# Four norm and score steps one slot later, and the last chunk's joined-sum products in another order

## The chip, the core and the metric

The kernel runs on one core of a Trainium2 chip. The metric is the device time of one execution in microseconds (us), as the median of several runs. Before the change it is 802.1 us, the median of four runs: 802.75, 802.56, 801.64 and 801.57 us.

The engines are named as in the profile: PE (matrix products; its weight loads are PEld), DVE (vector), ACT (scalar functions and copies), POOL (general elementwise work, and issuing of some transfers) and SP (issuing of transfers only). Each engine works through its own instructions in order; engines wait for one another through semaphores.

## What is computed

Two parts in sequence: an attention over channels, and a gated feed-forward layer on its result.

```
qn = q / (norm of q over N + 1e-6);  kn likewise       # q, k, v: 4 x 6016 x 256
s  = kn.T @ qn / tau;  s = s - max;  a = exp(s);  a /= a.sum(-1) + 1e-9   # 4 x 256 x 256
x  = (v @ a) as 24064 x 256
out = (sigmoid(x @ w_gate) * (x @ w_val)) @ w_out       # w_gate, w_val: 256 x 1536; w_out: 1536 x 256
```

So per batch there is a 256 x 256 matrix `a`, and the product `v @ a @ w_gate` can be had as `v @ (a @ w_gate)`: the kernel folds `a` into the weights once per batch.

## The kernel before

**Tiling.** A batch has 47 row tiles of 128 rows. They are taken in 12 chunks (`ci` 0 to 11), eleven of four tiles (512 rows) and a last one of three (384 rows). A chunk has 12 slots (`f` 0 to 11), one for each 128 of the 1536 hidden features. All four batches run one after the other, so there are 4 x 12 x 12 = 576 slots.

**One slot** (`glu`, L640 on). PE makes `ps_gate` (two matmuls), then a share of the product work for the chunk before (`run_work`), then `ps_val` (two matmuls). ACT turns `ps_gate` into `g_sb` (L660). DVE joins `g_sb` with `ps_val` into `hT` (L663). `ps_gate` and `ps_val` have two buffers each, so the `ps_val` matmuls of a slot need the L663 of two slots before.

**Products with fewer multiplications.** For a chunk of four tiles, `hT @ w_out` is made from seven block products instead of eight (a Strassen scheme), for two pairs `p` = 0 and 1 of tiles. The products read either `hT` itself or sums of its blocks. `a_sum` (L674) makes these *joined sums* on DVE, for each half of the features in three steps: step 0 (L689, the diagonal sum, read by product `z1`), step 1 (L691, read by `x2` and `y2`) and step 2 (L693, the differences, read by `z2` and `v2`). The first half's steps run in slots 7, 9 and 11 of the chunk itself (`OWN_SLOTS`), the second half's in slots 0, 2 and 4 of the next chunk (`NEXT_SLOTS`). Slots 1, 3, 5, 6, 8 and 10 have no joined sum.

`ORDER` is the order of the fourteen products (seven for each pair), six matmuls each, 84 in all; `run_work` deals them out over the next chunk's slots, seven to a slot, and about eight to a slot in the very last chunk. After `z1` of a pair, `part` (L742 to L744) copies three blocks out of PSUM on ACT and adds them on POOL; after `v2`, `whole` (L749 to L760) does the rest. Products `x2`, `y2`, `z2` and `v2` are added onto the blocks that `part` has read, so they have to come after its copy.

**The next batch's attention.** `side_work` puts steps for batch `n = b + 1` into slots of batch `b` by a slot number 0 to 143 (chunk times 12 plus slot). With `s0` = 98 the end of this chain, for `n` = 2 and 3, is: norms and a reciprocal square root (slots 105 on, DVE and POOL); `norms_inv` (L506 and L507 on DVE, 128x4) and `spread_both` (a DVE transpose, L458, and two POOL transfers `row<-rT`, L461) in slot 110; `read_row` (an SP transfer `rk_sb<-row`, L469) and `score_blocks` (eight POOL adds, L415) in slot 112; `scale_x` (L445, DVE) in slots 120 and 122; `exps` (L548, ACT) in 123 and 124; `all_sums` (five small matmuls into `ps_r` and a DVE reciprocal, L573) in 126; then twelve pieces of folded weights (`gh`: two matmuls into `ps_gh`, stored by ACT L607 or DVE L609) from slot 128 on. For `n` = 1 `norms_inv` is in slot 108 and `spread_both` in 109, there is no `score_blocks`, and the rest is the same. Slot 108 is slot 0 of chunk 9, slot 120 is slot 0 of chunk 10.

In a slot the instructions are issued in this order: `glu` with the products, the store of the chunk before last (slot 4 only), the joined sum of the slot, then the side work. All of this order is written out by hand.

Of the kernel before, what the change touches and what calls it, by code (L numbers as in the profile page):

```python
# [39 lines left out]
ORDER = (  # L40
    (0, "y1"), (1, "y1"), (0, "x1"), (0, "z1"), (1, "x1"), (1, "z1"),
    (0, "x2"), (0, "y2"), (0, "z2"), (0, "v2"),
    (1, "x2"), (1, "y2"), (1, "z2"), (1, "v2"),
)
NEXT_SLOTS = {0: 0, 2: 1, 4: 2}

FREE_SLOTS = (1, 3, 5, 6, 8, 10)
SCORE_SLOTS = {0: (1, 3, 6, 8, 10), 4: (2, 4, 6, 9, 11), 8: (0, 2, 5, 7, 10)}
GH_SLOTS = (128, 130, 131, 133, 135, 137, 138, 140, 142, 145, 147, 149)
OWN_SLOTS = {7: 0, 9: 1, 11: 2}  # L50


# [1 line left out]
def kernel(  # L54
# [26 lines left out]
    B, N, C = q.shape  # L81
# [592 lines left out]
    def a_sum(b, ci, g, m):  # L674

        nt = groups[ci][1]
        half = nt // 2
        hT = hts[b, ci]
        if (b, ci, g) not in sums:
            sums[b, ci, g] = spool.tile(  # L680
                [P, 5, FC // 4, CH // 2], BF16, tag=f"s{g}", name="sums", bufs=2 - g
            )
        f0, f1 = g * (FC // 2), (g + 1) * (FC // 2)
        n = half * P
        first, count = A_STEPS[m]
        out = sums[b, ci, g][:, first : first + count, :, :n].rearrange("p m j n -> p j m n")
        x = hT[:, f0:f1, : 2 * n].rearrange("p (j k) (r n) -> p j k r n", k=2, r=2)
        if m == 0:
            nc.vector.tensor_tensor(out=out[:, :, 0], in0=x[:, :, 0, 0], in1=x[:, :, 1, 1], op=ALU.add)  # L689
        elif m == 1:  # L690
            nc.vector.tensor_tensor(out=out, in0=x[:, :, 0], in1=x[:, :, 1], op=ALU.add)  # L691
        else:
            nc.vector.tensor_tensor(out=out, in0=x[:, :, :, 0], in1=x[:, :, :, 1], op=ALU.subtract)  # L693
# [9 lines left out]
    def out_work(b, ci):  # L703

        nt = groups[ci][1]
        half = nt // 2
        hT = hts[b, ci]
        work = []
        states = [{} for _ in range(half)]
        singles = {}  # L710
        plain = (b, ci) == (0, 0)

        def product(p, name, i):
            state = states[p]
            region, a, w = PRODUCTS[name]
            first = name == "y1" and i == 0
            if first:
                state["ps"] = pso.tile([P, CH], FP32, tag="o", name="ps_o")
            g, j = divmod(i, FC // 4)
            if isinstance(a, tuple):  # L720
                lhsT = hT[:, 2 * i + a[1], ds((a[0] * half + p) * P, P)]
            else:
                lhsT = sums[b, ci, g][:, a, j, ds(p * P, P)]
            rhs = w_out_sb[:, 2 * i + w[0], ds(w[1] * P, P)] if isinstance(w, tuple) else w_sums[:, w, i, :]
            mm(
                state["ps"][:, ds(region * P, P)],
                lhsT,
                rhs,
                start=first,
                stop=(i == FC // 2 - 1),  # L730
                skip_group_check=True,
            )
            if i == FC // 2 - 1:
                if name == "z1":
                    part(p)
                elif name == "v2":
                    whole(p)

        def part(p):

            m = states[p]["m"] = mpool.tile([P, 3, P], FP32, tag="m", name="m_sb")
            nc.scalar.copy(m, states[p]["ps"][:, : 3 * P].rearrange("p (n c) -> p n c", c=P))  # L742
            nc.gpsimd.tensor_tensor(out=m[:, 1, :], in0=m[:, 1, :], in1=m[:, 2, :], op=ALU.add)  # L743
            nc.gpsimd.tensor_tensor(out=m[:, 2, :], in0=m[:, 1, :], in1=m[:, 0, :], op=ALU.add)  # L744

        def whole(p):

            o = out_tile(b, ci)
            nc.scalar.copy(  # L749
                o[:, p : p + half + 1 : half, :],  # L750
                states[p]["ps"].rearrange("p (t c) -> p t c", c=C),
            )
            blocks = o.rearrange("p t (h c) -> p (t h) c", c=P)
            c00, c11 = 2 * p, 2 * (half + p) + 1
            ends = blocks[:, c00 : c11 + 1 : c11 - c00, :]
            mids = blocks[:, c00 + 1 : c11 : max(1, c11 - c00 - 2), :]
            last = (b, ci) == (B - 1, NCH - 2)
            add = nc.gpsimd.tensor_tensor
            add(out=ends, in0=ends, in1=states[p]["m"][:, 1:3, :], op=ALU.add)  # L759
            add(out=ends, in0=ends, in1=mids, op=ALU.subtract)  # L760
            if last:
                t0 = groups[ci][0]
                nc.sync.dma_start(out=out_rows[b][:, t0 + p : t0 + nt : half, :], in_=o[:, p:nt:half, :])
            elif p == half - 1:
                stores.append((b, ci))

        def single(s, f):
            if f == 0:
                singles[s] = pso.tile([P, CH], FP32, tag="o", name="ps_o")
            ps = singles[s]  # L770
            mm(ps[:, :C], hT[:, f, ds(s * P, P)], w_out_sb[:, f, :], f == 0, f == FC - 1)
            if f == FC - 1:
                nc.scalar.copy(out_tile(b, ci)[:, s, :], ps[:, :C])
                if plain and s == nt - 1:
                    stores.append((b, ci))

        if plain:
            return [(2, single, t, f) for t in range(nt) for f in range(FC)]
        for p, name in ORDER:
            if p < half:  # L780
                for i in range(FC // 2):
                    work.append((1, product, p, name, i))
                if nt % 2 and name == "z1":
                    for f in range(FC):
                        work.append((2, single, nt - 1, f))
        return work
# [126 lines left out]
    def side_work(b):  # L913
# [4 lines left out]
        def at(slot, fn, *a):  # L918
            side.setdefault(divmod(slot, FC), []).append((fn, a))
# [14 lines left out]
        n = b + 1  # L934
# [35 lines left out]
        if b == 0:  # L970
            at(s0 - 4, acc_fold, n, 0, (2, 1))
            at(s0 + 1, acc_fold, n, 1, (2, 1))
            at(s0 + 3, norms_mm, n)
            at(s0 + 4, root_seed, n)
            at(s0 + 4, root_steps, n)
            at(s0 + 10, norms_inv, n)
            at(s0 + 11, spread_both, n)
            at(s0 + 13, read_row, n)
        else:
            at(s0 - 4, acc_fold, n, 1, (4,))  # L980
            at(s0 - 1, acc_fold, n, 1, (2, 1))
            at(s0 + 3, acc_fold, n, 0, (4,))
            at(s0 + 4, acc_fold, n, 0, (2, 1))
            at(s0 + 5, score_out, n, 0)
            at(s0 + 7, norms_mm, n)
            at(s0 + 7, score_out, n, 1)
            at(s0 + 7, root_seed, n)
            at(s0 + 7, root_steps, n)
            at(s0 + 12, norms_inv, n)
            at(s0 + 12, spread_both, n)  # L990
            at(s0 + 14, read_row, n)
            at(s0 + 14, score_blocks, n)
        at(s0 + 22, scale_x, n, 0)
        at(s0 + 24, scale_x, n, 1)
        at(s0 + 25, exps, n, 0)
        at(s0 + 26, exps, n, 1)
        at(s0 + 28, all_sums, n)
        at(s0 + 28, gh_tiles, n)
        for i, piece in enumerate(gh_order):
            slot = GH_SLOTS[i]  # L1000
# [17 lines left out]
    for b in range(B):  # L1018
        side = side_work(b)
        for ci in range(NCH):  # L1020
            final = (b, ci) == (B - 1, NCH - 1)
            for f in range(FC):
                mid = gh_mid.get(f) if (b, ci) == (0, 0) else None
                if prev is not None:
                    mid = lambda: run_work(work, 1 / max(1, FC - final - f))
                elif mid is not None:
                    mid = lambda ns=mid: gh_pieces(ns)
                glu(b, ci, f, mid)
                if prev is not None:
                    if f == 4:  # L1030
                        store()
                    if f in NEXT_SLOTS and prev != (0, 0):
                        a_sum(*prev, 1, NEXT_SLOTS[f])
                if f in OWN_SLOTS and not final and (b, ci) != (0, 0):
                    a_sum(b, ci, 0, OWN_SLOTS[f])
                for fn, a in spill.get((b, ci, f), []) + side.get((ci, f), []):
                    fn(*a)
                if (b, ci) == (0, 0):
                    gh_pieces(gh_end.get(f, ()))
            prev = (b, ci)  # L1040
            if not final:
                work = out_work(*prev)
# [39 lines left out]
```

## Time and profile before

The profiled execution took 802.75 us, of which the span from its first to its last instruction is 800.7 us; 2.05 us lie around it. Its TensorE clock was granted at 0.998 of full speed.

| what | value |
|---|---|
| median of four runs | 802.1 us (801.57 to 802.75) |
| profiled execution | 802.75 us |
| its span | 800.7 us |
| DVE busy | 682.0 us (85% of the span) |
| ACT busy | 512.7 us (64%) |
| POOL busy | 408.8 us (51%) |
| one L663 of 512 columns, mean | 683 ns |
| one joined sum of step 0, 1, 2, mean | 559, 953, 1072 ns |
| L506 of `r_wide`, three of them | 689 to 696 ns |
| L507, L458 | 178, 209 ns |
| L445 from PSUM (batch 1), from SBUF (batches 2, 3) | 473 ns, 670 to 945 ns |

The busy share of an engine is an average; what a step costs is read from the slot it stands in. A useful yardstick is the distance between the first `ps_gate` matmuls of two neighbouring slots. In the timeline an idle time in front of an instruction is in square brackets with what ended it.

### The profile page before, as it was taken

To read this page: it belongs to the slowest core of one execution; us is meant where nothing else is said; L and a number is where in the kernel's file an instruction comes from. 1 tells how busy PE (TensorE), PEld (TensorE's weight loads), DVE (VectorE), ACT (ScalarE), POOL (GpSimd) and SP (SyncE) were. 2 spreads that over 40 slices of the span, in tenths; PEclk is the share of its full clock that TensorE was granted. 3 is DMA by queue.
4 is the path that set the end of the run, shared out by engine and by line. 5 is a ranking of instruction groups with operands and counts; after the bars stand their busy time and mean duration, and the time that the engine had idled before them with its cause. 6 is when DMAs were issued, how large, how long until landed. Compare 5 with 4: busy or idle time off the path is not lost.

```text
span 800.7 us, 18098 instructions
## 1 busy us (share of the span) xinstructions
PE 781.9 (98%) x6875; PEld 498.8 (62%) x6875; DVE 682.0 (85%) x1056; ACT 512.7 (64%) x891; POOL 408.8 (51%) x633
## 2 busy tenths in 40 slices
PE   4899999999999999999999999999999999999998
PEld 2546666666666666666666666666666666666666
DVE  5767898898889999899989999999888888888885
ACT  3766777766667767665667776766665565565563
POOL 3566455346553666554843565654754234334333
PEclk9999999999999999999999999999999999999999
DMA  9997858532685897752486599856234423423302
GB/s 214 189 205 123 139 96 141 95 66 54 131 142 105 148 180 149 138 101 53 101 147 123 103 177 164 152 114 107 54 65 86 68 54 83 78 54 81 72 27 73
DMA packets 85303, 89.12 MB, mean 111 GB/s; under 512 B 52704, under 2 KB 58464, under 8 KB 85216
## 3 DMA queue, kind: packets, MB, share of 16 engines
q0 software_dynamic: 28144, 49.82, 37.2%
q1 hardware_dynamic: 56496, 37.30, 21.2%
q8 instruction: 53, 0.87, 0.4%
q10 hardware_dynamic: 576, 0.85, 0.3%
q14 instruction: 34, 0.28, 0.1%
HBM read 79.04 MB, written 24.64 MB: 129 GB/s over the span
## 4 chain that ended last, share of the span: by engine, by line
PE 94%; DMA 4%; POOL 1%; DVE 0%; issue 0%; POOLq 0%; DVEq 0%
PE ps_val L129 30%; PE ps_gate L129 30%; PE ps_o L129 27%; PE ps_s L129 4%; DMA qk_sb<-in_k_dram 3%; PE ps_gh L129 2%; DMA w_gate<-in_moe_w_gate_dram 1%; POOL w_gate L208 0%; POOL w_val L208 0%; POOL qk_sb L148 0%; PE ps_end L129 0%; DVE hT L663 0%; POOL v_sb L160 0%; DVE sums L689 0%; DVE sums L693 0%
## 5 line engine op out<-in xcount | busy, mean ns | idle before, releaser
L660 ACT ACTIVATE g_sb<-ps_gate 128x512 f32<-128x512 f32 (+1 forms) x576 | 338.4, 588 | 248.9 <-PE ps_gate L129 237.7
L663 DVE SCALAR_TENSOR_TENSOR hT<-g_sb,ps_val 128x512 bf16<-128x512 f32 (+1 forms) x576 | 385.9, 672 | 98.5 <-PE ps_val L129 69.7
L129 PE MATMUL ps_gate<-vT,gh_G 128*128 128x512 bf16 (+1 forms) x1152 | 337.6, 375 | 0.0
L129 PE MATMUL ps_val<-vT,gh_H 128*128 128x512 bf16 (+1 forms) x1152 | 337.5, 375 | 0.1
L129 PEld LDWEIGHTS <-sums 128*128 128x128 bf16 x2670 | 183.0, 98 | 82.4 <-DVE sums L689 0.3
L759 POOL TENSOR_TENSOR out_sb<-out_sb,m_sb 128x256 f32<-128x256 f32 x89 | 69.1, 777 | 202.5 <-ACT out_sb L749 175.0
L129 PEld LDWEIGHTS <-gh_G 128*128 128x128 bf16 x1152 | 104.2, 98 | 82.3 <-DVE gh_G L609 0.3
L129 PE MATMUL ps_o<-w_sums,sums 128*128 128x128 bf16 x1602 | 154.6, 219 | 0.2 <-DVE sums L689 0.2
L129 PEld LDWEIGHTS <-hT 128*128 128x128 bf16 x1200 | 88.4, 98 | 46.8
L743 POOL TENSOR_TENSOR m_sb<-m_sb 128x128 f32<-128x128 f32 x89 | 49.6, 557 | 130.0 <-ACT m_sb L742 129.8
L760 POOL TENSOR_TENSOR out_sb<-out_sb 128x256 f32<-128x256 f32 x89 | 93.4, 1049 | 7.0
L129 PE MATMUL ps_o<-w_out_sb,sums 128*128 128x128 bf16 x1068 | 96.2, 219 | 0.0
L129 PE MATMUL ps_o<-w_sums,hT 128*128 128x128 bf16 x1068 | 95.5, 219 | 0.0
L693 DVE TENSOR_TENSOR sums<-hT 128x1536 bf16<-128x1536 bf16 (+1 forms) x92 | 95.5, 1038 | 0.0
L129 PEld LDWEIGHTS <-gh_H 128*128 128x128 bf16 x1152 | 90.2, 98 | 3.7 <-DVE gh_H L609 0.3
L691 DVE TENSOR_TENSOR sums<-hT 128x1536 bf16<-128x1536 bf16 (+1 forms) x92 | 85.6, 931 | 0.0
L129 PEld LDWEIGHTS <-qk_sb 128*128 128x128 bf16 x286 | 30.3, 106 | 42.6 <-issue 9.6
L749 ACT COPY out_sb<-ps_o 128x512 f32<-128x512 f32 x89 | 51.7, 580 | 0.0
L689 DVE TENSOR_TENSOR sums<-hT 128x768 bf16<-128x768 bf16 (+1 forms) x92 | 51.6, 561 | 0.0
L744 POOL TENSOR_TENSOR m_sb<-m_sb 128x128 f32<-128x128 f32 x89 | 46.3, 521 | 7.0
L129 PE MATMUL ps_s<-qk_sb 128*128 128x256 bf16 (+1 forms) x194 | 36.1, 308 | 13.9 <-ACT qk_sb L195 7.0
L256 ACT ACTIVATE sq<-qk_sb 128x1024 bf16<-128x1024 bf16 (+3 forms) x36 | 35.7, 1011 | 12.0 <-DMA qk_sb<-in_k_dram 12.0
(104 smaller groups left out, 552.8 us busy)
## 6 DMA issues: line engine op xcount, KB each, us to landing
out_dram<-out_sb SPq DMA_DIRECT2D x43, 512.0 KB, 3.4
v_sb<-in_v_dram POOLq DMA_DIRECT2D x44, 256.0 KB, 5.4
acc<-sq POOLq DMA_DIRECT2D x36, 256.0 KB, 4.9
qk_sb<-in_q_dram POOLq DMA_DIRECT2D x35, 256.0 KB, 7.3
qk_sb<-in_k_dram POOLq DMA_DIRECT2D x35, 256.0 KB, 6.2
qk_sb<-in_q_dram POOLq DMA_DIRECT2D x4, 512.0 KB, 11.6
qk_sb<-in_k_dram POOLq DMA_DIRECT2D x4, 512.0 KB, 13.5
w_f<-in_moe_w_out_dram POOLq DMA_DIRECT2D x3, 512.0 KB, 10.9
```

What stands on the lines that cost most here:

```text
L129: nc.tensor.matmul(out, lhsT=lhsT, rhs=rhs, start=start, stop=stop, **kw)
L256: nc.scalar.activation(out=sq[:, :nt, :], in_=src[:, :nt, :], func=ACT.Square)
L660: nc.scalar.activation(out=g_sb[:, :n], in_=ps_gate[:, :n], func=ACT.Tanh, scale=0.5)
L663: nc.vector.scalar_tensor_tensor(out=hts[b, ci][:, f, :n], in0=g_sb[:, :n], scalar=1.0, in1=ps_val[:, :n], op0=ALU.add, op1=ALU.mult,)
L689: nc.vector.tensor_tensor(out=out[:, :, 0], in0=x[:, :, 0, 0], in1=x[:, :, 1, 1], op=ALU.add)
L691: nc.vector.tensor_tensor(out=out, in0=x[:, :, 0], in1=x[:, :, 1], op=ALU.add)
L693: nc.vector.tensor_tensor(out=out, in0=x[:, :, :, 0], in1=x[:, :, :, 1], op=ALU.subtract)
L743: nc.gpsimd.tensor_tensor(out=m[:, 1, :], in0=m[:, 1, :], in1=m[:, 2, :], op=ALU.add)
L744: nc.gpsimd.tensor_tensor(out=m[:, 2, :], in0=m[:, 1, :], in1=m[:, 0, :], op=ALU.add)
L749: nc.scalar.copy(o[:, p : p + half + 1 : half, :], states[p]["ps"].rearrange("p (t c) -> p t c", c=C),)
L759: add(out=ends, in0=ends, in1=states[p]["m"][:, 1:3, :], op=ALU.add)
L760: add(out=ends, in0=ends, in1=mids, op=ALU.subtract)
```

## The change

Four things. First, `norms_inv` goes one slot later in all three batches that it is done for (slot 108 to 109 for `n` = 1; 110 to 111, with `spread_both`, for `n` = 2 and 3), and with it `read_row` and `score_blocks` (112 to 113, `n` = 2 and 3 only). Second, `scale_x`, `exps` and `all_sums` go one slot later each (120 and 122 to 121 and 123; 123 and 124 to 124 and 125; 126 to 127), and the first `gh` piece from 128 to 129. Third, for the last chunk of four tiles (batch 3, chunk 10), whose products run in the very last chunk, the order of products changes: the `x1` of pair 1 goes ahead of the `z1` of pair 0. Fourth, in the very last chunk the second half's step 2 (L693) goes from slot 4 to slot 3. No instruction is added or taken out.

```diff
+LAST_ORDER = ORDER[:3] + (ORDER[4], ORDER[3]) + ORDER[5:]
 NEXT_SLOTS = {0: 0, 2: 1, 4: 2}
+LAST_SLOTS = {0: 0, 2: 1, 3: 2}
...
-GH_SLOTS = (128, 130, 131, 133, 135, 137, 138, 140, 142, 145, 147, 149)
+GH_SLOTS = (129, 130, 131, 133, 135, 137, 138, 140, 142, 145, 147, 149)
...
-        for p, name in ORDER:
+        for p, name in LAST_ORDER if (b, ci) == (B - 1, NCH - 2) else ORDER:
...
-            at(s0 + 10, norms_inv, n)
+            at(s0 + 11, norms_inv, n)
             at(s0 + 11, spread_both, n)
             at(s0 + 13, read_row, n)
...
-            at(s0 + 12, norms_inv, n)
-            at(s0 + 12, spread_both, n)
-            at(s0 + 14, read_row, n)
-            at(s0 + 14, score_blocks, n)
-        at(s0 + 22, scale_x, n, 0)
-        at(s0 + 24, scale_x, n, 1)
-        at(s0 + 25, exps, n, 0)
-        at(s0 + 26, exps, n, 1)
-        at(s0 + 28, all_sums, n)
+            at(s0 + 13, norms_inv, n)
+            at(s0 + 13, spread_both, n)
+            at(s0 + 15, read_row, n)
+            at(s0 + 15, score_blocks, n)
+        at(s0 + 23, scale_x, n, 0)
+        at(s0 + 25, scale_x, n, 1)
+        at(s0 + 26, exps, n, 0)
+        at(s0 + 27, exps, n, 1)
+        at(s0 + 29, all_sums, n)
         at(s0 + 28, gh_tiles, n)
...
-                    if f in NEXT_SLOTS and prev != (0, 0):
-                        a_sum(*prev, 1, NEXT_SLOTS[f])
+                    next_sums = LAST_SLOTS if final else NEXT_SLOTS
+                    if f in next_sums and prev != (0, 0):
+                        a_sum(*prev, 1, next_sums[f])
```

## Prediction

> **What bounds the kernel now.** I read the page's shares and its chain first, then what PE waited for.
>
> ```profile
> PE 781.9 (98%) x6875; PEld 498.8 (62%) x6875; DVE 682.0 (85%) x1056; ACT 512.7 (64%) x891; POOL 408.8 (51%) x633
> PE 94%; DMA 4%; POOL 1%; DVE 0%; issue 0%; POOLq 0%; DVEq 0%
> PE ps_o L129 <- DVE sums L689: 0.2, 1, 0.2
> ```
>
> PE sets the end. The change adds and removes no PE instruction, so it can only win idle time of PE, and the view of waits names hardly any: modelled matmul ends hide short ones. The distance between the first `ps_gate` matmuls of neighbouring slots shows them. In batch 3, chunks 1 to 10, it is 1.25 or 1.26 us throughout (chunk 10: 765.08 to 780.13, twelve slots, 15.05 us). Against that beat I went through all 576 slots in the timeline. The stages that the change touches:
>
> ```profile
> 567.45:582.68 15.23, 15.20 (x133) 9.43 (x132) 13.27 (x22) 8.85 (x17) 13.84 (x30) 1.00 0.32 71
> 582.68:599.24 16.56, 16.56 (x144) 10.13 (x143) 14.52 (x23) 10.46 (x20) 7.77 (x11) 1.00 0.30 65
> 765.08:780.13 15.05, 15.05 (x133) 9.38 (x132) 12.46 (x18) 8.86 (x17) 5.34 (x8) 1.00 0.09 36
> ```
>
> Rows: a stretch, its length, then busy time of PE, PEld, DVE, ACT, POOL, and the clock. Batch 2's chunk 9 (first row, the norms) is 15.23 - 15.05 = 0.18 us over the plain chunk; batch 1's has the same 0.18, batch 0's none. Chunk 10 (second row, the scores) holds 0.12 for `ps_r` and 3 x 0.43 for three `gh` pieces; 0.09 is left over, in slot 5 (1.34 instead of 1.25), in batches 1 and 2 and not in batch 0. The very last chunk's slots should be about 1.04 to 1.10; slot 2 is 1.44 and slot 6 is 1.27.
>
> How the 0.18 arises, batch 1, chunk 9:
>
> ```profile
> 379.59 0.69 DVE L663 SCALAR_TENSOR_TENSOR hT<-g_sb,ps_val 128x512 bf16<-128x512 f32 x1 [0.54 <-PE ps_val L129]
> 380.20 0.95 DVE L691 TENSOR_TENSOR sums<-hT 128x1536 bf16<-128x1536 bf16 x1
> 380.38 1.35 POOL L760 TENSOR_TENSOR out_sb<-out_sb 128x256 f32<-128x256 f32 x1
> 381.07 0.69 DVE L506 TENSOR_SCALAR r_wide<-r_wide 128x4 f32<-128x4 f32 x1
> ...
> 382.14 1.24 DVE L663 SCALAR_TENSOR_TENSOR hT<-g_sb,ps_val 128x512 bf16<-128x512 f32 x2
> 382.60 0.34 PEld L129 LDWEIGHTS <-gh_H 128*128 128x128 bf16 x2
> 382.84 0.59 PE L129 MATMUL ps_val<-vT,gh_H 128*128 128x512 bf16 x2
> ```
>
> After slot 2's joined sum come L506, L507 and L458 (381.07 to 382.22), so slot 3's L663 starts at 382.14 though its `ps_val` was ready at 380.73. Slot 5's `ps_val` needs that buffer: its weight loads last 0.34 instead of 0.15, the 0.19 that PE stands. L506, four elements wide, takes 0.69 and ends at 381.76, just as POOL's L760 ends at 381.73 (186.56 + 0.99 against 186.88 + 0.69, and 573.62 against 573.66, in the other batches); the same operation on `r`, with POOL quiet, takes 0.17.
>
> The last chunk's two waits:
>
> ```profile
> 782.59 0.61 DVE L689 TENSOR_TENSOR sums<-hT 128x768 bf16<-128x768 bf16 x1
> 783.25 0.17 PEld L129 LDWEIGHTS <-sums 128*128 128x128 bf16 x3 [0.34 <-DVE sums L689]
> ...
> 786.70 0.95 DVE L693 TENSOR_TENSOR sums<-hT 128x1536 bf16<-128x1536 bf16 x1
> 787.71 0.28 PEld L129 LDWEIGHTS <-sums 128*128 128x128 bf16 x5 [0.17 <-DVE sums L693]
> ```
>
> Eight products a slot bring `z1` of pair 0 into slot 2, where its fourth matmul stands 0.34 for the second half's diagonal sum; `z2` of pair 0 stands 0.17 for the differences.
>
> **The change, part by part.**
>
> **Norms, `n` = 2 and 3 (110 to 111).** Slot 3's L663 now directly follows L691: 381.07 to 381.75, 1.07 earlier, so slot 5's `ps_val` (382.65 on the beat) is free. Next late is slot 4's L663: L506 + L507 + L458 stand before it, 0.17 + 0.18 + 0.21 = 0.56, or 0.69 + 0.39 = 1.08 if POOL blocks again. It starts at 382.25 to 382.8, ends by 382.9 to 383.45; slot 6's `ps_val` wants it at 383.91. Behind it L693 (1.06) and slot 5's L663 (0.68) end by 384.6 to 385.2; slot 7's `ps_val` is due at 385.17. So the new stall is 0 to 0.05. I take the short price, because L760 is over when L506 comes; what POOL does then is the issue of `v_sb` (381.68 to 382.29), and L507 ran beside that in its usual 0.18. Gain 2 x 0.18 = 0.36.
>
> [...]
>
> *Queues.* On POOL, the two `row` transfers (1.10) pass behind pair 0's L743 and L744 (0.45 to 1.03 each), and the eight L415 (385.16 to 388.82) behind pair 1's two. POOL works through a backlog from 379.6 to 394, so the order changes and the sum doesn't: `row` goes out 0.7 to 1.9 later. SP's L469 waits for it (issue 386.97 now, landing 3.1 later, so 390.1), and behind it SP holds the `vT` transpose L626 (387.47), which is needed at 407.35. `rk_sb` arrives by 390.8 to 392.0 and the scores by about 390.5; `scale_x` comes for them at 394.3. Cost 0. Were that cover gone, DVE would stand, and PE after it.
>
> **Norms, `n` = 1.** Slot 0 to slot 1 of chunk 9, `spread_both` unmoved. Slot 1's L663 is free at 186.88 instead of 187.70; slot 2's starts at 188.1 (188.5 with the long L506) instead of 188.41, L691 behind it ends by 189.7 to 190.1, slot 3's L663 by 190.7, before slot 5's `ps_val` at 191.03. No wait was there, none comes: 0.
>
> **Scores.** Now `scale_x` of slot 2 holds slot 3's L663 back:
>
> ```profile
> 395.78 0.95 DVE L691 TENSOR_TENSOR sums<-hT 128x1536 bf16<-128x1536 bf16 x1
> 396.65 0.67 DVE L445 SCALAR_TENSOR_TENSOR x_sb<-x_sb,r_wide,rk_sb 128x256 f32<-128x256 f32 x1
> 397.25 0.68 DVE L663 SCALAR_TENSOR_TENSOR hT<-g_sb,ps_val 128x512 bf16<-128x512 f32 x1
> 397.36 0.51 ACT L548 ACTIVATE e_sb<-x_sb,shift 128x256 bf16<-128x256 f32 x1 [1.20 <-DVE x_sb L445]
> 397.83 0.24 PEld L129 LDWEIGHTS <-gh_H 128*128 128x128 bf16 x2
> ```
>
> Slot 5's `ps_val` waits for it: weight loads 0.24 instead of 0.15. Moved, L445 (0.47 to 0.95) comes after slot 3's L663, ends by 397.4 to 397.95; slot 4's L663 ends by 398.05 to 398.55 (slot 6's `ps_val` due 399.13), L693 and slot 5's L663 by 399.65 to 400.15 (slot 7's due 400.39). On ACT, L548 still waits for L445, with slot 5's L660 queued behind it, and behind that pair 1's copy L742 (0.47) and the second L548: L660 of slot 5 ends by 398.5 to 399.0 (slot 7's `ps_gate` due 399.57), that of slot 6 by 400.1 to 400.6 (slot 8's due 400.95). Both ends fit: gain 2 x 0.09 = 0.18, bound 0 to 0.18 by the thin 0.24. Batch 1's scores (L445 from PSUM, 0.47) had no wait; slot 6's `ps_val` has a slot to spare: 0.
>
> `ps_r`'s five matmuls (0.12) and the first `gh` piece (0.43) lengthen slots 7 and 9 instead of 6 and 8; L573 (0.18) comes behind slot 7's L689, 0.69 + 0.55 + 0.18 = 1.42 against a slot of 1.38, caught up in slot 8, which has no sum. The third piece needs the first's PSUM bank at slot 11, stored by ACT (0.69) two slots before: 0.
>
> **Last chunk, order.** `x1` of pair 1 fills slot 2; `z1` of pair 0 reaches its fourth matmul at about 783.95, after the sum's 783.20: gain 0.34, all later times 0.34 earlier. In exchange its copy L742 (0.48) falls behind slot 3's L660 (ends 784.43), runs until 784.91, and `x2` of pair 0, which overwrites what it reads, is due at 785.06. A handover took 0.05 (783.20 to 783.25): 0.10 to spare. Were that L660 a wide one (0.60), 0.07 would be lost.
>
> **Last chunk, differences.** L693 runs at 785.6 to 786.6 instead of 786.70 to 787.65; `z2` needs it at 787.2: gain 0.17. Late next is slot 4's L663, by 0.6, ending 787.1; slot 6's `ps_val` is due at 787.49. If pair 0's L744 comes in between on POOL, as beside L691 (1.05), 0.45 more: 0.1 lost at most.
>
> **Sum.** 0.36 + 0.18 + 0.34 + 0.17 = 1.05 us; what follows the last slot is one PE chain (`ps_o`, `ps_end`) and moves along. Span 800.7 - 1.05 = 799.65; profiled execution 802.75 - 1.05 = 801.70; this execution was the slowest of four, so from the median 802.1: **801.05 us**.
>
> **Rivals.**
>
> *The batches' waits only move on.* For: in chunk 9 the new L506 meets POOL's issue, margins of -0.03 and 0.24 at the long ends. Against: the beat is met at both ends. Only the last chunk wins, 0.51: 801.6.
>
> *Nothing comes of it.* The copy's 0.10 of slack in the last chunk fails, and POOL's adds stretch L693, beside the first rival: 802.1.
>
> *The row comes late, slower.* Place: POOL's queue before L461, SP's L469, then L445 on DVE at 394.3. PE stands when slot 4's `ps_val` (396.63) misses slot 2's L663: L445 must begin by 395.4, so from a landing 5.3 us later than now each us costs one, twice. At 7.0: 2 x 1.7 - 1.05 = +2.35, 804.45. For: `row`'s landing varies from 1.8 to 4.2 in this trace, and SP has stood 12.05 for it. Against: I find 1.9 of delay at most.
>
> **How the numbers follow.** Forecast 0.62, moved waits 0.20, nothing 0.11, late row 0.07. About 0.2%, 1.6 us, is what a measurement of this kernel can tell from no change. 1.05 is below that. The four runs lie from 801.57 to 802.75; a median from the lower end gives 801.57 - 1.05 = 800.52, at the bound of 800.5, so I give faster 0.30, nearly all of it from the forecast, same 0.63, slower 0.07 (the late row). Range: 800.52 less 0.3 for scatter, 800.2, up to 802.1, the no-gain case, which leaves out half of it and the late row.
>
> **What would show it.** Slot 5 of chunk 9 at 1.25 in batches 1 and 2, slot 5 of chunk 10 at 1.25, slots 2 and 6 of the last chunk at 1.10, L506 near 0.17, `rk_sb` before 392.0. A slot over its beat right behind a moved step, an L506 of 0.6, or DVE idle before L445 would make it wrong.

## The result, and the profile after

The changed kernel takes 800.71 us (median of 42 runs, 800.31 to 803.9); the kernel before 801.8 us (median of 63 runs, 801.28 to 803.76). The medians lie 1.09 us apart; the ratio on record is 0.9989, with a 95% interval from 0.9984 to 0.9993, which is 0.88 us less, from 0.56 to 1.28. Forecast were 801.05 us and 1.05 us less. The gain is clear of zero and smaller than the 0.2% that was named as the bound.

The profiled execution took 800.31 us with a span of 798.5, which is 2.2 us below the 800.7 of the profiled execution before. Only half of that belongs to the change. Before, the first chunk took 15.79 us (36.83 to 52.62), and the timeline shows PE's weight loads idle there twice for the transfers of `w_gate` (0.88 and 0.70); in the profile after it took 14.84 and began 0.16 earlier. Together this is 1.11 us of scatter in the start of the program. In the traces of other kernels, too, the start varies: the first `ps_gate` comes at 36.67 us in the profile after, at 36.83 in the one before, at 36.76 with the exps left and at 37.64 with the norms and the first `scale_x` moved. Whether it spreads all runs isn't shown, as most have no trace. To leave the start out, all comparisons below take the stretch from the first `ps_gate` of chunk 1 to the first `ps_gate` of the last slot: 739.87 us before, 738.81 after, **1.06 us less**.

Batch 1's chunks 9 and 10 and the very last chunk, after the change (columns: stretch, length, busy time of PE, PEld, DVE, ACT, POOL, clock, transfers):

```profile
374.45:389.50 15.05, 15.05 (x134) 9.39 (x133) 12.75 (x22) 8.86 (x17) 13.85 (x30) 1.00 0.32 71
389.50:405.97 16.47, 16.47 (x145) 10.09 (x143) 14.63 (x24) 10.56 (x20) 9.76 (x15) 1.00 0.72 129
778.48:791.37 12.89, 12.89 (x137) 9.75 (x136) 9.82 (x16) 8.06 (x17) 6.67 (x9) 1.00 0.17 63
```

15.23 became 15.05, 16.56 became 16.47, 13.41 became 12.89 (the last slot's end set 1.05 after its first matmul in both). PE's busy time equals the length in each row, but that proves little: it did so in chunk 10 before, too (16.56 and 16.56), where slot 5 stood 0.09. The slots show it. Slot 5 of chunk 9 is 1.25 now in batches 1 and 2 (1.44 before), slot 5 of chunk 10 1.25 (1.34), slots 2 and 6 of the last chunk 1.10 and 1.10 (1.44 and 1.27). Of all slots in the stretch, only these changed by more than 0.01, besides slots 6 to 9 of chunk 10, where `ps_r` and the first `gh` piece moved from one slot to the next. Lines moved down by two, so L506 is L508 now, L663 is L665 and L445 is L447.

The timeline of batch 1's chunk 9 answers to the lines shown before:

```profile
379.08 0.95 DVE L693 TENSOR_TENSOR sums<-hT 128x1536 bf16<-128x1536 bf16 x1
379.27 1.35 POOL L762 TENSOR_TENSOR out_sb<-out_sb 128x256 f32<-128x256 f32 x1
379.95 0.68 DVE L665 SCALAR_TENSOR_TENSOR hT<-g_sb,ps_val 128x512 bf16<-128x512 f32 x1
380.55 0.17 DVE L508 TENSOR_SCALAR r_wide<-r_wide 128x4 f32<-128x4 f32 x1
380.57 0.61 POOL L162 DMA_DIRECT2D v_sb<-in_v_dram  x1
...
381.10 0.65 DVE L665 SCALAR_TENSOR_TENSOR hT<-g_sb,ps_val 128x512 bf16<-128x512 f32 x1
381.49 0.15 PEld L131 LDWEIGHTS <-gh_H 128*128 128x128 bf16 x2
```

Slot 3's L665 follows the joined sum at once, the norm's addition takes 0.17 instead of 0.69, and the weight loads of slot 5's `ps_val` last 0.15: no wait. POOL's L762 ends at 380.62, and L508, whose record starts at 380.55, follows a L665 that ends at 380.63: the add is over, but only by 0.01. `rk_sb` goes out at 385.81 (SP's L471) and lands at most 3.0 later, by 388.8; the first `scale_x` comes for it at 393.31.

In the last chunk, the diagonal sum (L691) and the products that read it:

```profile
780.94 0.61 DVE L691 TENSOR_TENSOR sums<-hT 128x768 bf16<-128x768 bf16 x1
781.00 0.61 PE L131 MATMUL ps_o<-w_sums,hT 128*128 128x128 bf16 x8
...
782.10 0.61 PE L131 MATMUL ps_o<-w_sums,sums 128*128 128x128 bf16 x8
...
782.69 0.48 ACT L744 COPY m_sb<-ps_o 128x384 f32<-128x384 f32 x1
...
783.42 0.39 PE L131 MATMUL ps_o<-w_out_sb,sums 128*128 128x128 bf16 x4
...
783.85 0.95 DVE L695 TENSOR_TENSOR sums<-hT 128x1536 bf16<-128x1536 bf16 x1
```

Slot 2 now holds eight products of `hT`; `z1` runs in slot 3 without a gap, pair 0's copy L744 is over at 783.17, 0.25 before `x2` (the four matmuls at 783.42), and the differences L695 are ready at 784.80.

### The profile page after: what moved, and what is told of

Same layout as the page of the kernel before. It is cut to its first block, busy times and chain, and to the rows that moved or that the text cites. A ratio compares the mean times of both kernels' runs of the same rounds, so it can differ in the third digit from the quotient of the medians.

```text
span 798.5 us, 18098 instructions
## 1 busy us (share of the span) xinstructions
PE 778.9 (98%) x6875; PEld 498.1 (62%) x6875; DVE 680.9 (85%) x1056; ACT 512.9 (64%) x891; POOL 407.9 (51%) x633
## 4 chain that ended last, share of the span: by engine, by line
PE 95%; DMA 4%; DVE 0%; issue 0%; ACT 0%; POOL 0%; DVEq 0%; POOLq 0%
PE ps_gate L131 31%; PE ps_val L131 31%; PE ps_o L131 28%; DMA qk_sb<-in_k_dram 4%; PE ps_s L131 4%; PE ps_gh L131 3%; PE ps_end L131 0%; PE ps_n L131 0%; DVE x_sb L525 0%; PE ps_r L131 0%; ACT e_sb L543 0%; POOL qk_sb L150 0%; DVE x_sb L537 0%; DVE end L825 0%; DVE r L508 0%
## 5 line engine op out<-in xcount | busy, mean ns | idle before, releaser
L662 ACT ACTIVATE g_sb<-ps_gate 128x512 f32<-128x512 f32 (+1 forms) x576 | 338.4, 588 | 248.0 <-PE ps_gate L131 237.6
L665 DVE SCALAR_TENSOR_TENSOR hT<-g_sb,ps_val 128x512 bf16<-128x512 f32 (+1 forms) x576 | 386.7, 672 | 98.2 <-PE ps_val L131 69.4
L761 POOL TENSOR_TENSOR out_sb<-out_sb,m_sb 128x256 f32<-128x256 f32 x89 | 69.1, 776 | 203.2 <-ACT out_sb L751 175.7
L745 POOL TENSOR_TENSOR m_sb<-m_sb 128x128 f32<-128x128 f32 x89 | 48.1, 540 | 130.3 <-ACT m_sb L744 130.1
L762 POOL TENSOR_TENSOR out_sb<-out_sb 128x256 f32<-128x256 f32 x89 | 93.4, 1049 | 7.0
L695 DVE TENSOR_TENSOR sums<-hT 128x1536 bf16<-128x1536 bf16 (+1 forms) x92 | 96.1, 1044 | 0.0
L693 DVE TENSOR_TENSOR sums<-hT 128x1536 bf16<-128x1536 bf16 (+1 forms) x92 | 86.2, 937 | 0.0
L691 DVE TENSOR_TENSOR sums<-hT 128x768 bf16<-128x768 bf16 (+1 forms) x92 | 51.4, 559 | 0.0
L746 POOL TENSOR_TENSOR m_sb<-m_sb 128x128 f32<-128x128 f32 x89 | 45.9, 515 | 7.0
```

Of the source, the lines that this page charges most:

```text
L662: nc.scalar.activation(out=g_sb[:, :n], in_=ps_gate[:, :n], func=ACT.Tanh, scale=0.5)
L665: nc.vector.scalar_tensor_tensor(out=hts[b, ci][:, f, :n], in0=g_sb[:, :n], scalar=1.0, in1=ps_val[:, :n], op0=ALU.add, op1=ALU.mult,)
```

## Experiments

Nine kernels, all compared by the stretch defined above and by the lengths of slots (distance between the first `ps_gate` matmuls of neighbours), because single parts of 0.2 us lie below what the run times can tell: their ratios to the kernel before all have intervals of about plus or minus 0.001. Each kernel has one trace, but these lengths repeat: outside chunks 9 and 10 of batches 0 to 2 and the last chunk, the stretch is 632.41 in all eleven traces, within 0.005. Chunk lengths are those of batches 1 and 2; the last chunk is measured to the first matmul of its last slot, so 1.05 shorter than above.

| kernel | chunk 9 | chunk 10 | last chunk | stretch | against |
|---|---|---|---|---|---|
| before | 15.23, 15.23 | 16.56, 16.56 | 12.36 | 739.87 | |
| after | 15.05, 15.05 | 16.47, 16.47 | 11.84 | 738.81 | before: -1.06 |
| norms only | 15.05, 15.05 | 16.84, 16.84 | 12.37 | 740.08 | before: +0.21 |
| scores only | 15.24, 15.23 | 16.47, 16.47 | 12.37 | 739.70 | before: -0.17 |
| order only | 15.23, 15.23 | 16.55, 16.56 | 12.01 | 739.52 | before: -0.35 |
| differences only | 15.23, 15.23 | 16.55, 16.56 | 12.19 | 739.70 | before: -0.17 |
| L506 from PSUM | 15.05, 15.05 | 16.49, 16.48 | 12.36 | 739.36 | before: -0.51 |
| norms and first `scale_x` | 15.05, 15.05 | 16.48, 16.47 | 12.36 | 739.33 | before: -0.54 |
| `x2` right behind `z1` | 15.05, 15.05 | 16.47, 16.47 | 12.72 | 739.69 | after: +0.88 |
| row six slots late | 15.05, 15.06 | 18.29, 18.66 | 11.84 | 742.83 | after: +4.02 |
| exps left | 15.05, 15.05 | 16.87, 17.01 | 11.84 | 740.01 | after: +1.20 |

### The four parts alone

Norms only, on the kernel before:

```diff
-            at(s0 + 10, norms_inv, n)
+            at(s0 + 11, norms_inv, n)
...
-            at(s0 + 12, norms_inv, n)
-            at(s0 + 12, spread_both, n)
-            at(s0 + 14, read_row, n)
-            at(s0 + 14, score_blocks, n)
+            at(s0 + 13, norms_inv, n)
+            at(s0 + 13, spread_both, n)
+            at(s0 + 15, read_row, n)
+            at(s0 + 15, score_blocks, n)
```

> The kernel before with only the norms' steps a slot later (norms_inv, spread_both, read_row, score_blocks). My theory (three small DVE instructions behind a joined sum, the first held up by POOL): L506 falls from 0.69 to 0.17 us, slot 5 of chunk 9 goes from 1.44 to 1.25 us in batches 1 and 2, and the twelve slots of those chunks from 15.23 to 15.05; slot 5 of chunk 10 keeps its 1.34, the last chunk its 13.41. In all 0.36 us less. Rival (the waits only move on): L506 stays near 0.69 beside POOL's issue of v_sb, and another slot of chunk 9 goes over 1.25 by 0.1 or more.

Chunk 9 went as expected (L506 159 ns in the mean, 15.05). Chunk 10 did not: its slot 3 took 1.47 and its slot 5 1.41 instead of 1.25 and 1.34, so that this part alone makes the stretch **0.21 longer**. DVE at the start of batch 1's chunk 10 in the kernel before, and DVE and POOL at the same place in the norms-only kernel:

```profile
391.67 1.06 DVE L693 TENSOR_TENSOR sums<-hT 128x1536 bf16<-128x1536 bf16 x1
393.25 0.54 DVE L689 TENSOR_TENSOR sums<-hT 128x768 bf16<-128x768 bf16 x1
393.72 0.94 DVE L445 SCALAR_TENSOR_TENSOR x_sb<-x_sb,r_wide,rk_sb 128x256 f32<-128x256 f32 x1
394.59 1.27 DVE L663 SCALAR_TENSOR_TENSOR hT<-g_sb,ps_val 128x512 bf16<-128x512 f32 x2
```

```profile
390.48 1.35 DVE L693 TENSOR_TENSOR sums<-hT 128x1536 bf16<-128x1536 bf16 x1
391.75 0.67 DVE L663 SCALAR_TENSOR_TENSOR hT<-g_sb,ps_val 128x512 bf16<-128x512 f32 x1
392.35 0.54 DVE L689 TENSOR_TENSOR sums<-hT 128x768 bf16<-128x768 bf16 x1
392.49 0.99 POOL L760 TENSOR_TENSOR out_sb<-out_sb 128x256 f32<-128x256 f32 x1
392.82 0.94 DVE L445 SCALAR_TENSOR_TENSOR x_sb<-x_sb,r_wide,rk_sb 128x256 f32<-128x256 f32 x1
393.68 1.27 DVE L663 SCALAR_TENSOR_TENSOR hT<-g_sb,ps_val 128x512 bf16<-128x512 f32 x2
```

DVE never rests here, in either kernel. L693 of slot 11 takes 1.35 instead of the 1.06 of the kernel before, beside POOL's adds, which come about 0.3 later in the chunk than before: the eight score adds L415 in front of them meet slot 9's joined sum now and take 4.4 us instead of 3.7; then L689, then L445 with 0.94. Slot 1's L663 comes 0.28 later in its chunk than before (393.68 - 389.60 = 4.08 against 394.59 - 390.79 = 3.80); slot 3's `ps_val`, which needs its buffer, had only a little to spare, and slot 3 pays 0.22. L445 shows no idle time before it, so neither the row nor the scores were late.

Scores only:

```diff
-        at(s0 + 22, scale_x, n, 0)
-        at(s0 + 24, scale_x, n, 1)
-        at(s0 + 25, exps, n, 0)
-        at(s0 + 26, exps, n, 1)
-        at(s0 + 28, all_sums, n)
+        at(s0 + 23, scale_x, n, 0)
+        at(s0 + 25, scale_x, n, 1)
+        at(s0 + 26, exps, n, 0)
+        at(s0 + 27, exps, n, 1)
+        at(s0 + 29, all_sums, n)
```

(and the first entry of `GH_SLOTS` 129 instead of 128)

> The kernel before with only scale_x, exps, all_sums and the first gh piece a slot later. My theory: slot 5 of chunk 10 goes from 1.34 to 1.25 us in batches 1 and 2 and the chunk from 16.56 to 16.47; chunk 9 keeps its 15.23, the last chunk its 13.41; in all 0.18 us less. Rival (the waits move on, by L660 queued behind the later exps on ACT): slot 6, 7 or 8 of chunk 10 grows by about 0.1 over its beat and the sum stays at 16.56.

The times are as the theory has them: slot 5 of chunk 10 at 1.25 or 1.26, slots 6 to 8 on their beat (slot 7 is 1.38 with `ps_r`), 0.17 less.

Order only (`LAST_ORDER` of the change, nothing else) and differences only (`LAST_SLOTS`, nothing else):

> The kernel before with only the last chunk's order of products changed. My theory: slot 2 of the last chunk goes from 1.44 to 1.10 us, slot 6 keeps 1.27 (its wait for L693 moves along), the chunk is 13.07 instead of 13.41: 0.34 us less. Rival (x2 of pair 0 now waits for the copy L742): slot 4 grows from 1.11 by 0.1 to 0.3.

> The kernel before with only the last chunk's differences (L693) in slot 3. My theory: slot 6 of the last chunk goes from 1.27 to 1.10 us, slot 2 keeps 1.44, the chunk is 13.24 instead of 13.41: 0.17 us less. Rival (the later L663 of slot 4 holds up slot 6's ps_val): slot 6 stays above 1.2.

Order only: slot 2 at 1.10, slot 6 still 1.27, 0.35 less. Differences only: slot 2 still 1.44, slot 6 at 1.10, 0.17 less. Both rivals fall.

### Why a four-element instruction took 0.69 us

On the kernel before, in the old slot, with the source in PSUM (the squared norms; their square roots are left out of the scores). If it is the source in SBUF that ties L506 to POOL, it should take about 0.17 here, and slot 5 of chunk 9 1.25 instead of 1.44; that was the author's estimate, 0.36 us less in all without any move:

```diff
-        nc.vector.tensor_scalar(out=r, in0=r, scalar1=1e-6, scalar2=None, op0=ALU.add)
+        src = st[b]["n"] if "sq_n" in st[b] else r
+        nc.vector.tensor_scalar(out=r, in0=src, scalar1=1e-6, scalar2=None, op0=ALU.add)
```

> The kernel before, with L506 reading the squared norms from PSUM instead of their roots from SBUF (the roots are left out, so the scores are scaled otherwise); same instruction, same shape, same slot. [...] Rival (L506 waits for POOL by a semaphore or by its place, not by its source): it keeps 0.69 and the slot its 1.44.

```profile
381.22 0.95 DVE L692 TENSOR_TENSOR sums<-hT 128x1536 bf16<-128x1536 bf16 x1
381.41 1.34 POOL L761 TENSOR_TENSOR out_sb<-out_sb 128x256 f32<-128x256 f32 x1
382.08 0.15 DVE L507 TENSOR_SCALAR r_wide<-ps_s 128x4 f32<-128x4 f32 x1
...
382.62 1.24 DVE L664 SCALAR_TENSOR_TENSOR hT<-g_sb,ps_val 128x512 bf16<-128x512 f32 x2
```

The instruction is in the same place beside the same POOL add (381.41 to 382.75) and takes 0.15 instead of 0.69. Slot 5 of chunk 9 is 1.25: the wait is gone without any move. So it was the SBUF source, and not the place or a semaphore, that tied L506 to POOL; by what path in the chip, no run shows. Not foreseen: chunk 10 lost most of its wait too (16.49 and 16.48), in slot 5 (1.27 instead of 1.34), with both `scale_x` in their old slots. Its trace shows how. POOL has moved forward there: its L761 ends at 394.56, before the first L445 begins at 394.96, which takes 0.47, while in the kernel before L760 runs until 394.39, and L445, begun at 393.72, takes 0.94; its four from SBUF take 0.57 in the mean, 0.81 before.

### What chunk 10 needs

The norms' steps as in the change, and of the scores' steps the first `scale_x` alone:

```diff
-        at(s0 + 22, scale_x, n, 0)
+        at(s0 + 23, scale_x, n, 0)
```

> The kernel before with the norms' steps a slot later and, of the scores' steps, only the first scale_x (slot 120 to 121). Theory of a pile-up (in the norms-only kernel slot 11's L693, slot 0's L689 and the first L445 stand in a row on DVE, and POOL's shifted adds make L693 0.29 longer): with L445 out of the row, slot 3 of chunk 10 falls from 1.47 to 1.25 us in batches 1 and 2; slot 5, which is the second scale_x's, stays at 1.34 to 1.41; the chunk is 16.56 to 16.63. Rival (the scores or the row arrive late and L445 waits for them): slot 3 stays above 1.4, or L445 shows an idle time before it.

```profile
391.33 1.35 DVE L693 TENSOR_TENSOR sums<-hT 128x1536 bf16<-128x1536 bf16 x1
...
393.20 0.54 DVE L689 TENSOR_TENSOR sums<-hT 128x768 bf16<-128x768 bf16 x1
393.67 0.67 DVE L663 SCALAR_TENSOR_TENSOR hT<-g_sb,ps_val 128x512 bf16<-128x512 f32 x1
394.27 0.47 DVE L445 SCALAR_TENSOR_TENSOR x_sb<-x_sb,r_wide,rk_sb 128x256 f32<-128x256 f32 x1
```

L693 still takes 1.35, but slot 1's L663 no longer waits for L445, which takes 0.47, as POOL's add is over 0.06 after its start. Slot 3 is 1.25: the pile-up is confirmed. The expectation for slot 5 was wrong: it is 1.25 as well, though the second `scale_x` still stands in slot 2 behind its joined sum. DVE works without a rest from slot 11's L693 to slot 3's L663, with both `scale_x` in the row, so slot 5's wait ends by whatever brings that L663 forward: it starts 6.45 into the chunk in the kernel before (wait 0.09), 6.39 with L506 from PSUM (0.02) and 6.27 here (none). No run moves the second `scale_x` alone. Norms and first `scale_x` together bring 0.54, all that was forecast for the batches (0.36 + 0.18); the second `scale_x`, the exps, `all_sums` and the `gh` piece needn't have moved for it.

On the changed kernel, the exps left in their old slots:

```diff
-        at(s0 + 26, exps, n, 0)
-        at(s0 + 27, exps, n, 1)
+        at(s0 + 25, exps, n, 0)
+        at(s0 + 26, exps, n, 1)
```

> The changed kernel with exps left where they were (slots 123 and 124), so that the first exp stands in the same slot as the second scale_x. If ACT's order is what the later exps are good for: L550 waits on ACT for L447 with slot 4's L662 behind it, which starts about 1.3 us later than now, L665 of slot 4 follows about 1.1 later, and slot 7 of chunk 10 (or slot 6) grows by about 0.4 us in each of batches 1 and 2, maybe in batch 0 as well: 0.8 to 1.2 us more than the changed kernel. Rival (ACT has the time to spare, the exps needn't have moved): chunk 10 stays at 16.47 and no slot changes.

```profile
394.72 0.47 ACT L744 COPY m_sb<-ps_o 128x384 f32<-128x384 f32 x1
396.62 0.51 ACT L550 ACTIVATE e_sb<-x_sb,shift 128x256 bf16<-128x256 f32 x1 [1.42 <-DVE x_sb L447]
397.03 0.58 ACT L662 ACTIVATE g_sb<-ps_gate 128x512 f32<-128x512 f32 x1
```

With the second `scale_x` moved, the exps have to move too: the first exp stands on ACT for 1.42 with slot 4's L662 behind it, and chunk 10 takes 16.71, 16.87 and 17.01 in the three batches, 1.20 in all. The size was right; the place was slot 5 first (1.39 to 1.68) and slot 7 after it (1.49 or 1.50 instead of 1.38): `ps_gate` of slot 6 waits for the buffer that this L662 reads.

### Two limits that the change comes near

On the changed kernel, pair 0's `z1` behind pair 1's too:

```diff
-LAST_ORDER = ORDER[:3] + (ORDER[4], ORDER[3]) + ORDER[5:]
+LAST_ORDER = ORDER[:3] + (ORDER[4], ORDER[5], ORDER[3]) + ORDER[6:]
```

> The changed kernel, with pair 0's z1 put behind pair 1's z1 too, so that pair 0's x2 follows it at once. If x2 has to wait for the copy L744 of pair 0's blocks (my bound for the new order), PE stands before x2 in slot 4 of the last chunk until about 0.05 us after the copy, which comes behind that slot's L662: slot 4 takes about 2.1 us instead of 1.09, the chunk 13.9 instead of 12.89, 1.0 us more than the changed kernel. Rival (the copy is no limit, PE goes on): 12.9 us, no difference.

```profile
785.27 0.49 ACT L662 ACTIVATE g_sb<-ps_gate 128x384 f32<-128x384 f32 x1 [0.23 <-PE ps_gate L131]
785.66 0.47 ACT L744 COPY m_sb<-ps_o 128x384 f32<-128x384 f32 x1
786.18 0.38 PE L131 MATMUL ps_o<-w_out_sb,sums 128*128 128x128 bf16 x4 [0.72 <-ACT m_sb L744]
```

`x2` starts 0.05 after the copy's end (785.66 + 0.47 = 786.13), and slot 4 takes 1.98: 0.88 more. The copy is a limit of the order, and in the change it is met with room.

On the changed kernel, the norms' last steps six slots later in the second and third attention:

```diff
-            at(s0 + 13, norms_inv, n)
-            at(s0 + 13, spread_both, n)
-            at(s0 + 15, read_row, n)
+            at(s0 + 19, norms_inv, n)
+            at(s0 + 19, spread_both, n)
+            at(s0 + 21, read_row, n)
```

> The changed kernel, with norms_inv, spread_both and read_row six slots later for the second and third attention (slots 117 and 119), score_blocks left. By the prediction's late-row rival, PE loses from a landing of rk_sb of 5.3 to 5.6 us later than now, then one for one: POOL's queue puts row's issue at about 391 us in batch 1, rk_sb lands at about 397, L447 begins some 3.5 us late, and PE stands about 2.5 us in chunk 10 of batches 1 and 2, 5 us in all (2 to 6). Batch 0's chunks stay as they are. Rival (buffers take it up): less than 0.5 us in all.

```profile
388.60 1.33 POOL L762 TENSOR_TENSOR out_sb<-out_sb 128x256 f32<-128x256 f32 x1
389.27 0.69 DVE L508 TENSOR_SCALAR r_wide<-r_wide 128x4 f32<-128x4 f32 x1
...
392.99 0.33 SPq L471 DMA_DIRECT2D rk_sb<-row  x1
...
396.03 0.56 DVE L447 SCALAR_TENSOR_TENSOR x_sb<-x_sb,r_wide,rk_sb 128x256 f32<-128x256 f32 x1 [1.55 <-DMA rk_sb<-row]
...
397.24 0.59 PE L131 MATMUL ps_val<-vT,gh_H 128*128 128x512 bf16 x2 [0.90 <-DVE hT L665]
```

4.02 more, within the 2 to 6 expected; the time is 804.71 us, a ratio of 1.0034 to the kernel before, from 1.0020 to 1.0049. The prediction had PE standing once L445 begins later than 395.4, which is 4.61 into chunk 10. Here L447 begins 396.03 - 389.87 = 6.16 into it, and slot 0 is already 0.48 longer; 6.16 - 4.61 - 0.48 = 1.07, and slot 4 is 2.31 - 1.25 = 1.06 longer. In batch 2 the same sum gives 6.40 - 4.61 - 0.46 = 1.33 and slot 4 is 1.52 longer; its L447 took 0.77 where batch 1's took 0.56. The remaining loss (in batch 1, 0.48 in slot 0, 0.21 and 0.08 in slots 5 and 7) was not priced. L508 met POOL's L762 again and again ended with it (389.96 and 389.93).

## Why the prediction was right, and where it was not

- **The bound.** PE's beat, read slot by slot, named all that was won. The four losses named, 0.36, 0.18, 0.34 and 0.17, are the losses that went: by the slots, 0.37, 0.17, 0.34 and 0.17. The sum was 1.05, the stretch moved by 1.06.
- **Last chunk.** Both parts are what they were said to be, alone and together. The copy was over 0.25 before `x2` instead of 0.15, as ACT began it (782.69) 0.10 before the L662 ahead of it had ended (782.30 + 0.49). The price of a wide L660 there was added up wrongly: 0.60 - 0.49 is 0.11, which is 0.01 more than the 0.10 to spare, not 0.07. No run has this case.
- **Norms, slot and length.** L506 at 0.17, slot 3's L663 at once behind the sum: right, and the stall of up to 0.05 a batch that was weighed against it did not come. The margin is thin but steady: in all three cases in the profile after, POOL's add ended 0.011 to 0.013 before the L665 ahead of the moved step.
- **Norms, queues: the step that failed.** "The order changes and the sum doesn't", cost 0, was wrong as a price of this part. POOL's work moves against DVE's and does not keep its sum (L415 4.4 instead of 3.7), L693 of slot 11 grows from 1.06 to 1.35, and with the first `scale_x` still in slot 0 this costs 0.28 a batch in chunk 10, more than the 0.18 won. That it came out at nothing was luck of the combination: the change moves that `scale_x` as well, for another reason; in the profile after, L695 of slot 11 also takes 1.35. That L693 grows because POOL's adds work on SBUF beside it is the author's estimate from these times; a source in PSUM was tried on L506 only. The delay of the row was sized wrongly as well, without harm. POOL issued `row` 1.5 later in the chunk, inside the 0.7 to 1.9 forecast (8.43 into chunk 9 of batch 1 instead of 6.95), but SP's transfer, which waits for its landing, went out at 11.36 instead of 11.41, not later; why the landing did not move stays open.
- **Scores.** The gain was right and the cause was half of it: the prediction put slot 5's wait down to the second `scale_x` alone. The wait also ended (or all but ended, 0.02) with the second one in its old slot, once the first had left slot 0 or took 0.47 there.
- **The chances.** 0.63 for within 0.2% is where it fell (1.09 of 801.8 is 0.14%, and the ratio says 0.11%). Nothing in the runs spoke for the late row short of six slots' delay.

## What to carry to other kernels

Where one engine sets a steady beat, list the distance of its slots' first instructions and subtract the beat: waits too short for the view of waits show there, and their sum says what a reordering can bring that leaves the beat as it is: here 1.05 named, 1.06 won. Price moves together, not one by one: of two moves here one loses 0.21 us alone and wins with the other. When an instruction is moved later, see what its consumer then holds up on its own in-order queue: the exps left behind cost 1.20, while the first `scale_x`, moved with the exps left in place, cost nothing.

## What was not expected of the hardware

The addition on `r_wide`, a DVE instruction on four elements a row, took 0.69 us where it came during a POOL add on SBUF: 0.689 to 0.696 three times in the kernel before, 0.69 twice with the row six slots late, and in each of these five cases it ended 0.02 to 0.03 after that add. In the three kernels that leave it in its old slot, with its source in SBUF, its mean is 0.691 to 0.692. It took 0.158 to 0.166 in the profile after, between POOL's adds, and 0.15 in the mean with its source in PSUM. Two DVE instructions that read SBUF alone vary in the same company: L445 from 0.47 to 0.945, the joined sum of step 2 in slot 11 of batch 1's chunk 9 from 1.06 to 1.35. Whether POOL's issue of a transfer holds such an instruction as its adds do stays open: in the profile after, its record began 0.01 to 0.02 before that issue, all three times. The same addition on `r` at the start of the program points to it: in the profile after it took 0.28 (33.15 to 33.42) and ended with POOL's issue of `w_gate` (32.66 to 33.43). In the kernel before it took 0.17 (33.41 to 33.58), and POOL was not quiet then, as the prediction has it, but passed from one issue (to 33.48) to the next (from 33.41).
